# 512 rows of wq on 64 partitions, eight rows to a partition, contracted in eight steps of 64

## The chip, the cores and the metric

The kernel runs on one core of a Trainium2 chip. The core has five instruction streams: PE (TensorE, matmuls and their weight loads), DVE (VectorE), ACT (ScalarE), POOL (GpSimd) and SP (SyncE, which here issues nearly all loads). Sixteen DMA engines move data between the chip's memory (HBM) and SBUF, the 128-partition working memory. Matmuls read SBUF and write PSUM. The metric is the device time of one execution in microseconds (us).

## The reference: one decode step of a transformer block

Four sequences, one new token each, D = 576 features. The block is attention with a cached window and then a gated feed-forward layer, each behind a layer norm:

```python
q = (layernorm(x) @ wq)                      # [4, 576] @ [576, 32*128]
k = k_cache[:, :, Sk-4096:, :]               # 16 KV heads, 2 query heads for each
v = v_cache[:, :, Sk-4096:, :]
p = softmax(q . k * 128**-0.5)
h = x + (p . v) @ wo
h2 = h + (relu(hn @ W_gate) * (hn @ W_up)) @ W_down     # hn = layernorm(h)
```

Everything is bfloat16. The caches' windows are 4 x 16 x 4096 x 128 values each, 67 MB for K and 67 MB for V; wq and wo have 4.7 MB each, the three matrices of the feed-forward layer 5.3 MB each. Some 160 MB are read for each execution. This case is about the first product, layernorm(x) @ wq, and about how wq is brought into SBUF.

## The kernel before, in words

**Recording.** There is no automatic scheduler. Each engine's program is a Python function (`prog_sync`, `prog_act`, `prog_dve`, `prog_pe`, `prog_pool`), and an instruction is given the names of those it depends on. The class `Sched` runs all programs twice: first to number the names, then to emit, where a name becomes a wait on a semaphore's value. The order on an engine is the order written in its function. A wait that an engine has already made for the same or a higher value of the same counter is left out.

**SBUF as a pool.** All large loads go to one buffer, `pool`, of 65,536 bfloat16 columns on 128 partitions (128 KB each), used as four slots of `QUAD` = 16,384 columns. One K or V "quad" is four KV heads of one sequence, 4096 KB, and fills a slot: 128 partitions x 32 KB. There are 16 quads of K and 16 of V. `add` (line 203) puts a load on the list `transfers` and works out which earlier users of the same columns it has to wait for. K and V take the slots in turn, in the order K0, K1, V0, K2, V1, K3, ... (line 238): K0 has slot 0, K1 slot 1, V0 slot 2, K2 slot 3, V1 slot 0 again. The weights wo, W_gate, W_up and W_down come after the last V.

**The order of loads.** `prog_sync` issues `transfers` in order on SP's queue, one after the other, and waits ahead of each for the users of its columns. The first entries are the last 64 rows of wq (line 234, 512 KB, two half rows on 128 partitions, at the start of slot 3), the first 512 rows of wq (line 236, 4096 KB, all of slot 2), then the K and V quads. Since slots 0 and 1 are free at the start, K0 and K1 are issued without a wait. V0 (slot 2) and K2 (slot 3) wait for "QMM", the last matmul with wq. V1 waits until K0 has been transposed, and so on.

**The product with wq.** Partition p holds rows 4p to 4p+3 of wq (512 rows as 128 x 4). The normalized x, `xn_bf` (4 x 576), is turned by PE with five transposes (`turn`, line 473; `feat(c)` picks the features c, c+4, c+8, ...), and ACT copies the result to `xnT` (line 311, features 0 to 511) and `x4` (line 310, the last 64). A small matmul with `dup` spreads the last 64 over 128 partitions ("XDUP", line 480). Then the loop of line 481 goes over the row steps c: first c = 4, the last 64 rows, which need only the smaller load, then c = 0 to 3, each contracting over 128 partitions. For each c there are eight matmuls of 512 columns (4 groups g of 32 PSUM partitions, 2 banks k). The groups g write different 32-column strips of the array. A matmul with k = 1 is emitted without a weight load of its own (`held`). Line 464 is the matmul with a weight load and line 466 the held one; all matmuls of the kernel are recorded at these two lines, so in a profile they are told apart by their tiles.

**After the product.** ACT copies q to SBUF (line 320). DVE transposes the first part of K0 (line 402), then q (line 428). PE rearranges q, ACT builds the block-diagonal weights `qz` (line 336), and the loop over quads begins: four transposes of K on DVE, the scores on PE, the maximum on DVE, its reduction over partitions on POOL, the exponential on ACT, the transpose of the probabilities on DVE, and the product with V on PE.

Of the kernel before, what the change touches and what calls it, by code (L numbers as in the profile page):

```python
# [10 lines left out]
BF16 = mybir.dt.bfloat16  # L11

B = 4
D = 576
# [7 lines left out]
DC = 5  # L22
# [9 lines left out]
QUAD = NS * WIN * DH // 128  # L32
# [70 lines left out]
def bass_sequential_preLN__sliding_block_cached__glu_gated_reglu__decode_kernel(  # L103
# [12 lines left out]
    with ExitStack() as es:  # L116
        cnt = [0]

        def sb(name, shape, dt):
            return es.enter_context(nc.sbuf_tensor(name, shape, dt))  # L120

        pool = sb("pool", [128, NSLOT * QUAD], BF16)
        kT = sb("kT", [128, NKT, QUAD // 8], FP32)
        ident_b = sb("ident_b", [128, 128], BF16)
# [6 lines left out]
        x_bf = sb("x_bf", [B, D], BF16)  # L131
        xn_bf = sb("xn_bf", [B, D], BF16)
        st1 = sb("st1", [B, 20], FP32)
        xnT = sb("xnT", [128, 4, 32], BF16)
        xn4 = sb("xn4", [128, 2, 32], BF16)
        x4 = sb("x4", [64, B], BF16)
        dup = sb("dup", [64, 128], BF16)
# [37 lines left out]
        pb = [sc[:, i * 512:(i + 1) * 512] for i in range(4)]  # L175
# [4 lines left out]
        QB = (5, 6)  # L180
# [13 lines left out]
        tpv = pb[TPB].bitcast(BF16)  # L194

        S = Sched()
# [4 lines left out]
        at = {}  # L201

        def add(name, key, off, n, consumer, make):

            free = []
            for u in list(users):
                if u[0] < off + n and off < u[1]:
                    if u[2] not in free:
                        free.append(u[2])
                    if off <= u[0] and u[1] <= off + n:  # L210
                        users.remove(u)
            users.append((off, off + n, consumer))
            at[name] = off
            transfers.append((name, key, free, lambda e: make(e, pool[:, off:off + n])))
# [12 lines left out]
        def add_V(i):  # L227
# [3 lines left out]

        HQ = H * DH

        add(("wq", 4), "wq4", 2 * QUAD + 4 * HQ, HQ // 2, "QMM",
            lambda e, o: e.dma_start(out=o, in_=A_wq[512:576, :].rearrange("r (u n) -> (r u) n", u=2)))
        add(("wq", 0), "wq0", 2 * QUAD, 4 * HQ, "QMM",
            lambda e, o: e.dma_start(out=o, in_=A_wq[0:512, :].rearrange("(p u) n -> p (u n)", u=4)))
        for m in range(NQUAD + VLEAD):
            if m < NQUAD:
                add_K(m)  # L240
# [4 lines left out]
        for k, (kind, W) in enumerate((("wg", B_W_gate), ("wu", B_W_up))):  # L245
            add((kind, 0), f"{kind}0", GU0 + 4 * k * ROW, 4 * F, None,
                lambda e, o, W=W: e.dma_start(out=o, in_=W[0:512, :].rearrange("(p u) n -> p (u n)", u=4)))
            add((kind, 4), f"{kind}4", GU0 + 8 * ROW + k * HALF, HALF, None,
                lambda e, o, W=W: e.dma_start(out=o, in_=W[512:576, :].rearrange("r (u n) -> (r u) n", u=2)))
# [3 lines left out]
        for k, (f0, f1) in enumerate(WD):  # L253
            transfers.append((("wd", k), f"wd{k}", ["ATTN"],
                              lambda e, f0=f0, f1=f1: e.dma_start(
                                  out=pool[:, f0 * D:f1 * D], in_=B_W_down.rearrange("(p j) n -> p (j n)", j=JJ)[:, f0 * D:f1 * D])))

        def feat(c):
            return slice(c, c + 509, 4) if c < 4 else slice(512, D)

        def land(name):
            return ("L",) + (name if isinstance(name, tuple) else (name,))
# [38 lines left out]
        def prog_act(S):  # L301
            a = "scalar"
            S.dma(a, lambda e: e.dma_start(out=x_bf[:, :], in_=A_x.rearrange("b s d -> (b s) d")), "x", name=land("x"))
            S.op(a, lambda e: e.activation(out=st1[:, 14:15], in_=st1[:, 13:14], func=ACT.Sqrt, bias=eps_c[0:B, 0:1], scale=1.0),
                 deps=["D_VAR", "EPS"], name="A_STD")
            S.op(a, lambda e: e.copy(out=dup[:, :].rearrange("p (r u) -> p r u", u=2),
                                     in_=bass.AP(tensor=ident_b, offset=0, ap=[[128, 64], [1, 64], [0, 2]])), deps=["IDB"], name="DUP")
            S.op(a, lambda e: e.copy(out=col[:, :].rearrange("p (a s) -> p a s", s=NS),
                                     in_=bass.AP(tensor=ident_b, offset=0, ap=[[128, NS], [0, 128], [1, NS]])), name="COL")
            S.op(a, lambda e: e.copy(out=x4[:, :], in_=tpv[0:64, 16:20]), deps=["TP1"], name="D_X4")  # L310
            S.op(a, lambda e: e.copy(out=xnT[:, :, 0:B], in_=tpv[:, 0:16].rearrange("p (c b) -> p c b", b=B)), deps=["XNZ"], name="D_XNT")
            S.op(a, lambda e: e.activation(out=foe[:, :].rearrange("p (a s x) -> p a s x", s=NS, x=2),
                                           in_=bass.AP(tensor=ident_b, offset=0, ap=[[128, NS], [0, 16], [1, NS], [0, 2]]),
                                           func=ACT.Copy, scale=FAR, bias=-FAR), name="FOE")
            S.op(a, lambda e: e.activation(out=mask[:, 1, :], in_=mask[:, 0, :], func=ACT.Copy, scale=FAR, bias=-FAR), deps=["M0"], name="M1")
            for u in range(2):
                S.op(a, lambda e, u=u: e.activation(out=xn4[:, u, 0:B], in_=pb[STB][:, 0:B], func=ACT.Copy, scale=par[:, u:u + 1]),
                     deps=["XDUP", "PAR2", "XN4Z"], name=f"XN4{u}")
            for k in range(2):
                S.op(a, lambda e, k=k: e.copy(out=q_bf[:, k, :].rearrange("p (x e k) -> p x e k", e=2, k=32),  # L320
                                              in_=pb[QB[k]].rearrange("p (x k e) -> p x e k", e=2, k=32)), deps=["QMM"], name=f"QBF{k}")
            S.op(a, lambda e: e.copy(out=qrep[:, :, :].rearrange("p x (g y) -> p x g y", g=4),  # L322
                                     in_=sc.ap().rearrange("p (g r) -> p g r", g=4)[:, :, 0:128].rearrange("p g (x y) -> p x g y", x=4)),
                 deps=["QREP"], name="D_QR")
# [16 lines left out]
            for i in range(NQUAD):  # L341
                S.op(a, lambda e, i=i: e.activation(out=pmax[:, i % 2, :], in_=mask[:, 1, :], func=ACT.Identity, bias=rmx[:, i % 2:i % 2 + 1], scale=1.0),  # L342
                     deps=[("RMAX", i)], name=("EMAX", i))
                deps = [("BIAS", i)]
                if i >= 2:
                    deps.append(("TRP", i - 2))
                S.op(a, lambda e, i=i: e.activation(  # L347
                    out=Pb[:, (i % 2) * 1024:(i % 2 + 1) * 1024], in_=sc[:, (i % 2) * 1024:(i % 2 + 1) * 1024], func=ACT.Exp,
                    scale=SCALE, bias=bias[:, i % 2:i % 2 + 1], accum_out=rs1[:, i:i + 1]),
                    deps=deps, name=("EXP", i))  # L350
                if i + 2 < NQUAD:
                    qzero(i + 2)
            S.op(a, lambda e: e.copy(out=bass.AP(tensor=spread, offset=0, ap=[[16 * H, H], [4 * H + 1, 4], [4, H]]),
                                     in_=bass.AP(tensor=ident_b, offset=0, ap=[[128, H], [0, 4], [1, H]])),
                 deps=["SP0"], name="SPREAD")
            S.op(a, lambda e: e.copy(out=oX[:, :, :].rearrange("p e b -> p (e b)"), in_=pb[0][:, 0:EO * B]), deps=["OSEL"], name="OX")  # L356
            S.op(a, lambda e: e.activation(out=st2[:, 14:15], in_=st2[:, 13:14], func=ACT.Sqrt, bias=eps_c[0:B, 0:1], scale=1.0),
                 deps=["D_VAR2"], name="A_STD2")
            S.op(a, lambda e: e.copy(out=hnT[0:64, 4, 0:B], in_=tpv[0:64, 16:20]), deps=["TP2", "HN4Z"], name="N1")
            S.op(a, lambda e: e.copy(out=hnT[:, 0:4, 0:B], in_=tpv[:, 0:16].rearrange("p (c b) -> p c b", b=B)), name="N2")  # L360
            for u in range(2):
                S.op(a, lambda e, u=u: e.activation(out=hn4[:, u, 0:B], in_=pb[SUB][:, 400:400 + B], func=ACT.Copy, scale=par[:, u:u + 1]),
                     deps=["HDUP"], name=f"HN4{u}")
            for k, (f0, f1) in enumerate(CUTS):
                S.op(a, lambda e, k=k, f0=f0, f1=f1: e.activation(out=gate_sb[:, :, f0:f1].rearrange("p j f -> p f j"), in_=part(0, k, "f j"), func=ACT.Relu),
                     deps=[("GATE", k)], name=("RELU", k))
# [90 lines left out]
        def prog_pe(S):  # L457
            t = "tensor"

            def mm(o, l, r, start, stop, deps=(), name=None, skip=False, held=False):  # L460

                def make(e):
                    if not held:
                        return e.matmul(o, lhsT=l, rhs=r, start=start, stop=stop, skip_group_check=skip)  # L464
                    tile = tuple(next(x for x in (32, 64, 128) if x >= n) for n in (l.shape[0], l.shape[-1]))
                    return e.add_instruction(mybir.InstMatmult(  # L466
                        name=nc.get_next_instruction_name(), start_tensor_calc=start, stop_tensor_calc=stop, bass_skip_group_check=skip,
                        tile_size=tile, tile_position=(0, o.offset // o.ap[0][0] % 128), ldweights=False,
                        ins=[e.lower_ap(r), e.lower_ap(l)], outs=[e.lower_ap(o)]))

                S.op(t, make, deps=deps, name=name, signal=name is not None)

            def turn(src, deps, name):
                for c in range(DC):
                    w = 128 if c < 4 else 64
                    S.op(t, lambda e, c=c, w=w: e.transpose(out=tpv[0:w, c * 4:(c + 1) * 4], in_=src[0:B, feat(c)], identity=ident_b[0:B, 0:B]),
                         deps=deps if c == 0 else [], name=name if c == DC - 1 else None, signal=c == DC - 1)

            turn(xn_bf, ["XN", "IDB"], "TP1")
            mm(pb[STB][:, 0:B], dup[:, :], x4[:, :], True, True, deps=["D_X4", "DUP"], name="XDUP")  # L480
            for c in (4, 0, 1, 2, 3):
                s = at[("wq", 0)] + c * HQ if c < 4 else at[("wq", 4)]
                deps = [land(("wq", 0)), "D_XNT"] if c == 0 else [land(("wq", 4)), "XN41"] if c == 4 else []
                for g in range(4):
                    x0 = s + (g if c < 4 else g % 2) * 1024
                    for k in range(2):
                        mm(pb[QB[k]][32 * g:32 * g + 32, :], xnT[:, c, :] if c < 4 else xn4[:, g // 2, :], pool[:, x0 + 512 * k:x0 + 512 * k + 512], c == 4, c == 3,
                           deps=deps, name="QMM" if c == 3 and g == 3 and k == 1 else None, skip=True, held=k == 1)
                        deps = []
            for g in range(4):  # L490
                mm(pb[g][:, 0:128].rearrange("p (x h b) -> p x h b", x=4, b=B), sel[32 * g:32 * g + 32, :, :].rearrange("p g k -> p (g k)"),
                   qT[32 * g:32 * g + 32, :].rearrange("p (h x b) -> p x h b", x=4, b=32)[:, :, :, 0:B], True, True,
                   deps=["D_QT", "SEL"] if g == 0 else [], name="QREP" if g == 3 else None)
# [50 lines left out]
            for q in range(4):  # L544
                mm(pb[0][:, 0:EO * B], spread[:, q, :, :].rearrange("p h k -> p (h k)"), o_bf[:, q * EO:(q + 1) * EO, :].rearrange("p e b -> p (e b)"), q == 0, q == 3,
                   deps=["NORM", "SPREAD"] if q == 0 else [], name="OSEL" if q == 3 else None)
            for e_ in range(EO):
                deps = [land(("wo",)), "OX"] if e_ == 0 else []
                for u in range(2):
                    c0 = at[("wo",)] + e_ * D + u * HD  # L550
                    mm(attn[:, u * HD:(u + 1) * HD], oX[:, e_, :], pool[:, c0:c0 + HD], e_ == 0, e_ == EO - 1,
                       deps=deps, name="ATTN" if e_ == EO - 1 and u == 1 else None, held=u == 1)
                    deps = []
# [10 lines left out]
            for u, kind in ((0, "wg"), (1, "wu")):  # L564
                if u == 1:
                    residual()
                for c in range(4):
                    s = at[(kind, 0)] + c * F
                    deps = [land((kind, 0))] + (["N2"] if c == 0 and u == 0 else [])
                    for k, (f0, f1) in enumerate(CUTS):  # L570
                        for q in range(4):
                            x0 = s + q * FQ
                            mm(pb[GUB[u][k]][32 * q:32 * q + 32, 0:(f1 - f0) * JJ], hnT[:, c, :], pool[:, x0 + f0 * JJ:x0 + f1 * JJ],
                               c == 0, False, deps=deps, skip=True, held=k > 0)
                            deps = []
                s = at[(kind, 4)]
                deps = [land((kind, 4)), "HN41"]
                for k, (f0, f1) in enumerate(CUTS):
                    for q in range(4):
                        x0 = s + (q % 2) * FQ  # L580
                        mm(pb[GUB[u][k]][32 * q:32 * q + 32, 0:(f1 - f0) * JJ], hn4[:, q // 2, :], pool[:, x0 + f0 * JJ:x0 + f1 * JJ],
                           False, True, deps=deps, name=(("GATE", "GU")[u], k) if q == 3 else None, skip=True, held=k > 0)
                        deps = []

            for k, (f0, f1) in enumerate(WD):
                deps = [land(("wd", k))]
                for f in range(f0, f1):
                    if f % (JJ // 2) == 0:
                        deps = deps + [("HHT", f // (JJ // 2))]
                    for u in range(2):  # L590
                        last = f == FC - 1
                        mm(down(u), hhT[:, f, 0:B], wd_sb[:, f, OUTS[u][0]:OUTS[u][1]], False, last,
                           deps=deps, name="DOWN1" if last and u == 1 else None, skip=True)
# [37 lines left out]
```

## Time and profile before

| What | Value |
|---|---|
| median of 3 timed runs | 377.9 us (377.59 to 378.06) |
| profiled execution | 378.37 us |
| its span, first to last instruction | 377.0 us |
| mean granted TensorE clock | 0.923 |
| PE busy | 291.9 us (77%) |
| DVE busy | 222.5 us (59%) |
| ACT busy | 53.1 us (14%) |
| DMA, SP's queue | 159.59 MB, 98.7% of 16 engines' span |
| mean rate of all DMA | 424 GB/s |
| first 512 rows of wq, issue to landing | 13.6 us |
| last 64 rows of wq, issue to landing | 3.3 us |

Times in the profile are in us from the start of the span, unless marked ns. L236 means line 236 of the kernel. A line of the timeline has the start, the duration, the engine, the line, the operation, what it writes and reads, the count, and in brackets how long the engine was idle before and what ended that. The windows give, for stretches of the span, the busy time of each engine with the number of its instructions, the granted clock of TensorE, the mean busy share of the 16 DMA engines, and what they moved in GB/s. The share can pass 1.00 a little, because a packet is counted where it ends. SPq stands for DMA issues on SP. "Issue" time of a load and its landing are told apart: a load is issued in half a microsecond and lands when its last packet has.

### The profile page before, as it was taken

The numbers are of one execution on the slowest core, as the hardware profiler recorded it, in microseconds if no ns is written. First come the engines' busy times: TensorE is split into PE (matmuls) and PEld (weight loads), VectorE is DVE, ScalarE is ACT, GpSimd is POOL, SyncE is SP. The second block draws the span as 40 slices with busy tenths as digits, with TensorE's granted clock in tenths as the row PEclk, the third lists the DMA queues.
The fourth block names the chain that finished last, engine by engine and source line by source line (L and its number), as shares of the span: only waits on it lengthen the run. The fifth ranks groups of instructions, "written<-read, shape, count | busy, mean of one in ns | idle before, by whom it ended". The sixth has DMA issues, their size and how long they took to land.

```text
span 377.0 us, 2565 instructions
## 1 busy us (share of the span) xinstructions
PE 291.9 (77%) x1384; PEld 67.9 (18%) x740; DVE 222.5 (59%) x169; ACT 53.1 (14%) x138; POOL 12.1 (3%) x34
## 2 busy tenths in 40 slices
PE   1408299969996999499939996799689967977675
PEld 0001012212221222022202221122112211222213
DVE  3037577696859494859476856775676658221230
ACT  3003402010220012001200220021002010101020
POOL 6000000000000000000000000000000000000000
PEclk9999879998998799989998998999869995996989
DMA  8999999999999999999999999999999999999995
GB/s 334 431 445 441 403 438 440 441 418 424 437 441 428 414 441 436 435 410 441 441 426 421 435 445 428 431 422 441 431 435 415 441 435 428 447 428 416 418 417 245
DMA packets 6507, 159.74 MB, mean 424 GB/s; under 512 B 729, under 2 KB 865, under 8 KB 1633
## 3 DMA queue, kind: packets, MB, share of 16 engines
q1 hardware_dynamic: 6488, 159.59, 98.7%
q8 instruction: 8, 0.13, 0.1%
q14 instruction: 3, 0.02, 0.0%
q10 hardware_dynamic: 8, 0.00, 0.0%
HBM read 159.58 MB, written 0.00 MB: 423 GB/s over the span
## 4 chain that ended last, share of the span: by engine, by line
DMA 53%; DVE 28%; PE 15%; ACT 2%; issue 1%; SPq 1%; POOL 0%; DVEq 0%
DMA pool<-in_A_k_cache_dram 48%; DVE kT L402 19%; PE sc L464 5%; PE sc L466 5%; DMA pool<-in_B_W_down_dram 5%; DVE acc L421 4%; DVE own_sb L418 2%; PE val L464 2%; PE val L466 2%; DVE probT L415 1%; DVE rmx L405 1%; ACT P L347 1%; DVE o_bf L440 0%; ACT L347 0%; ACT qz L336 0%
## 5 line engine op out<-in xcount | busy, mean ns | idle before, releaser
L402 DVE STREAM_TRANSPOSE kT<-pool 128x2048 f32<-128x2048 f32 x64 | 142.9, 2279 | 34.9 <-DMA pool<-in_A_k_cache_dram 33.9
L464 PE MATMUL sc<-kT,qz 128*128 128x512 bf16 x240 | 104.4, 435 | 28.7 <-DVE kT L402 28.7
L466 PE MATMUL sc<-kT,qz 128*128 128x512 bf16 x256 | 110.4, 431 | 18.3 <-DVE kT L402 16.2
L464 PE MATMUL val<-pool,probT 128*64 128x512 bf16 (+2 forms) x328 | 102.4, 360 | 4.6 <-DMA pool<-in_B_W_down_dram 4.6
L466 PE MATMUL val<-pool,probT 128*64 128x512 bf16 x256 | 96.2, 379 | 0.0
L464 PEld LDWEIGHTS sc<-kT,qz 128*128 128x128 bf16 x256 | 26.9, 105 | 154.8 <-issue 76.3
L464 PEld LDWEIGHTS val<-pool,probT 128*64 128x64 bf16 (+1 forms) x328 | 31.4, 104 | 88.0 <-issue 78.1
L405 DVE TENSOR_REDUCE rmx<-sc 128x1 f32<-128x1024 f32 x16 | 19.6, 1225 | 42.4 <-PE sc L466 42.4
L342 ACT ACTIVATE pmax<-mask,rmx 128x8 f32<-128x8 f32 x16 | 4.8, 301 | 241.3 <-DVE rmx L405 241.3
L415 DVE STREAM_TRANSPOSE probT<-P 128x1024 bf16<-128x1024 bf16 x16 | 19.9, 1245 | 20.7 <-ACT P L347 20.7
L347 ACT ACTIVATE P<-sc,bias 128x1024 bf16<-128x1024 f32 x16 | 17.8, 1113 | 13.3 <-DVE bias L410 13.3
L336 ACT COPY qz<-qrep 32x128 bf16<-32x128 bf16 x64 | 18.8, 294 | 0.6
L294 POOL PARTITION_ALL_REDUCE bcm<-pmax x16 | 5.9, 367 | 312.8 <-ACT pmax L342 312.8
L421 DVE TENSOR_REDUCE acc<-own_sb 128x128 f32<-128x1024 f32 x8 | 15.2, 1895 | 0.3
L418 DVE TENSOR_TENSOR own_sb<-val,mask 128x1024 f32<-128x1024 f32 x8 | 9.5, 1193 | 8.3 <-PE val L466 8.3
L464 PE MATMUL sc<-pool,oX 128*4 128x288 bf16 x32 | 10.2, 345 | 0.4 <-ACT oX L356 0.4
L408 DVE SCALAR_TENSOR_TENSOR t<-bcm,mask 128x8 f32<-128x8 f32 x16 | 2.7, 167 | 13.3 <-POOL bcm L294 13.3
L466 PE MATMUL sc<-pool,oX 128*4 128x288 bf16 x32 | 10.2, 343 | 0.0
L464 PE MATMUL sc<-qT,sel 32*128 32x128 bf16 x4 | 0.3, 284 | 9.8 <-DVE qT L428 9.8
L443 DVE TENSOR_TENSOR h_row<-sc,x_bf 4x576 f32<-4x576 f32 x1 | 0.7, 745 | 11.9 <-PE sc L466 11.9
L464 PE MATMUL sc<-col,foe 4*128 4x512 bf16 x16 | 6.4, 399 | 0.7 <-ACT qrep L322 0.7
L464 PE MATMUL val<-pool,xnT 128*32 128x512 bf16 x16 | 2.6, 628 | 5.0 <-DMA pool<-in_A_wq_dram 5.0
(98 smaller groups left out, 74.4 us busy)
## 6 DMA issues: line engine op xcount, KB each, us to landing
pool<-in_A_k_cache_dram SPq DMA_DIRECT2D x16, 4096.0 KB, 26.9
pool<-in_A_v_cache_dram SPq DMA_DIRECT2D x16, 4096.0 KB, 26.8
pool<-in_A_wo_dram SPq DMA_DIRECT2D x1, 4608.0 KB, 18.3
pool<-in_B_W_gate_dram SPq DMA_DIRECT2D x1, 4608.0 KB, 17.8
pool<-in_B_W_up_dram SPq DMA_DIRECT2D x1, 4608.0 KB, 24.0
pool<-in_A_wq_dram SPq DMA_DIRECT2D x1, 4096.0 KB, 13.6
pool<-in_B_W_down_dram SPq DMA_DIRECT2D x1, 2016.0 KB, 13.7
pool<-in_B_W_down_dram SPq DMA_DIRECT2D x1, 1296.0 KB, 16.4
```

What stands on the lines that cost most here:

```text
L294: S.op(g, lambda e, i=i: e.partition_all_reduce(bcm[:, i % 2, :], pmax[:, i % 2, :], 128, bass_isa.ReduceOp.max), deps=deps, name=("PAR", i))
L336: S.op(a, lambda e, src=src, dst=dst: e.copy(out=dst, in_=src), deps=deps, name=("QZ", i) if g == 3 else None, signal=g == 3)
L342: S.op(a, lambda e, i=i: e.activation(out=pmax[:, i % 2, :], in_=mask[:, 1, :], func=ACT.Identity, bias=rmx[:, i % 2:i % 2 + 1], scale=1.0 ...
L347: S.op(a, lambda e, i=i: e.activation(out=Pb[:, (i % 2) * 1024:(i % 2 + 1) * 1024], in_=sc[:, (i % 2) * 1024:(i % 2 + 1) * 1024], func=ACT ...
L402: S.op(v, lambda e: e.transpose(out=dst, in_=src), deps=deps, name=("TR", f))
L405: S.op(v, lambda e: e.tensor_reduce(out=rmx[:, i % 2:i % 2 + 1], in_=sc[:, (i % 2) * 1024:(i % 2 + 1) * 1024], axis=AX.X, op=ALU.max), dep ...
L408: S.op(v, lambda e: e.scalar_tensor_tensor(out=t8[:, :], in0=bcm[:, i % 2, :], scalar=-SCALE, in1=mask[:, 0, :], op0=ALU.mult, op1=ALU.mul ...
L415: S.op(v, lambda e: e.transpose(out=pT[i % NPT], in_=Pb[:, (i % 2) * 1024:(i % 2 + 1) * 1024]), deps=[("EXP", i)] + ([("PV", i - NPT)] if ...
L418: S.op(v, lambda e: e.tensor_tensor(out=own_sb[:, :].rearrange("p (x d) -> p x d", d=DH), in0=val[:, :].rearrange("p (x d) -> p x d", d=DH ...
L421: S.op(v, lambda e: e.tensor_reduce(out=acc[:, w % 2, :], in_=own_sb[:, :].rearrange("p (x d) -> p d x", d=DH), axis=AX.X, op=ALU.add), de ...
L464: return e.matmul(o, lhsT=l, rhs=r, start=start, stop=stop, skip_group_check=skip)
L466: return e.add_instruction(mybir.InstMatmult(name=nc.get_next_instruction_name(), start_tensor_calc=start, stop_tensor_calc=stop, bass_ski ...
```

## The change

The first 512 rows of wq go to 64 partitions in place of 128. Partition p (0 to 63) holds rows 8p to 8p+7, which is 64 KB for a partition: the load (still one DMA of 4096 KB) now takes slots 2 and 3 of the pool, on their lower 64 partitions. The last 64 rows, which lay at the start of slot 3, move to the start of slot 1. By the bookkeeping of `add`, K1, which goes to slot 1, now has to wait for the last matmul with wq; V0 and K2 have to wait for the same matmul, as before.

The product goes over eight steps of 64 partitions in place of four of 128: 64 matmuls of 512 columns where there were 32, after the eight with the last 64 rows. `turn` gets a parameter `u`, the number of rows to a partition, and makes nine transposes of 64 features here in place of five (the second use, behind the second layer norm, keeps five). `xnT` is 64 x 8 x 32 in place of 128 x 4 x 32, and ACT's two copies read other columns of the transposes' PSUM bank. `feat` falls away, and with it three lines, so that line numbers behind it are three lower.

```diff
-        xnT = sb("xnT", [128, 4, 32], BF16)
+        xnT = sb("xnT", [64, 8, 32], BF16)
...
-        add(("wq", 4), "wq4", 2 * QUAD + 4 * HQ, HQ // 2, "QMM",
+        add(("wq", 4), "wq4", QUAD, HQ // 2, "QMM",
...
-        add(("wq", 0), "wq0", 2 * QUAD, 4 * HQ, "QMM",
-            lambda e, o: e.dma_start(out=o, in_=A_wq[0:512, :].rearrange("(p u) n -> p (u n)", u=4)))
+        add(("wq", 0), "wq0", 2 * QUAD, 8 * HQ, "QMM",
+            lambda e, o: e.dma_start(out=o[0:64, :], in_=A_wq[0:512, :].rearrange("(p u) n -> p (u n)", u=8)))
...
-            S.op(a, lambda e: e.copy(out=x4[:, :], in_=tpv[0:64, 16:20]), deps=["TP1"], name="D_X4")
-            S.op(a, lambda e: e.copy(out=xnT[:, :, 0:B], in_=tpv[:, 0:16].rearrange("p (c b) -> p c b", b=B)), deps=["XNZ"], name="D_XNT")
+            S.op(a, lambda e: e.copy(out=x4[:, :], in_=tpv[0:64, 32:36]), deps=["TP1"], name="D_X4")
+            S.op(a, lambda e: e.copy(out=xnT[:, :, 0:B], in_=tpv[0:64, 0:32].rearrange("p (c b) -> p c b", b=B)), deps=["XNZ"], name="D_XNT")
...
+            def turn(src, deps, name, u=4):
+                for c in range(u + 1):
+                    w = 512 // u if c < u else 64
+                    cols = slice(c, c + 512 - u + 1, u) if c < u else slice(512, D)
...
-            turn(xn_bf, ["XN", "IDB"], "TP1")
+            turn(xn_bf, ["XN", "IDB"], "TP1", u=8)
...
-            for c in (4, 0, 1, 2, 3):
+            for c in (8, 0, 1, 2, 3, 4, 5, 6, 7):
...
+                np_ = 64 if c < 8 else 128
...
-                        mm(pb[QB[k]][32 * g:32 * g + 32, :], xnT[:, c, :] if c < 4 else xn4[:, g // 2, :], pool[:, x0 + 512 * k:x0 + 512 * k + 512], c == 4, c == 3,
+                        mm(pb[QB[k]][32 * g:32 * g + 32, :], xnT[:, c, :] if c < 8 else xn4[:, g // 2, :], pool[0:np_, x0 + 512 * k:x0 + 512 * k + 512], c == 8, c == 7,
```

More of the change, by code (lines that the diff above doesn't have):

```diff
@@ L256, in bass_sequential_preLN__sliding_block_cached__glu_gated_reglu__decode_kernel @@
                                   out=pool[:, f0 * D:f1 * D], in_=B_W_down.rearrange("(p j) n -> p (j n)", j=JJ)[:, f0 * D:f1 * D])))
-        def feat(c):
-            return slice(c, c + 509, 4) if c < 4 else slice(512, D)
         def land(name):
@@ L471, in mm @@
                 S.op(t, make, deps=deps, name=name, signal=name is not None)
[L473 to L477, printed above, removed]
-            turn(xn_bf, ["XN", "IDB"], "TP1")
+            def turn(src, deps, name, u=4):
+                for c in range(u + 1):
+                    w = 512 // u if c < u else 64
+                    cols = slice(c, c + 512 - u + 1, u) if c < u else slice(512, D)
+                    S.op(t, lambda e, c=c, w=w, cols=cols: e.transpose(out=tpv[0:w, c * 4:(c + 1) * 4], in_=src[0:B, cols], identity=ident_b[0:B, 0:B]),
+                         deps=deps if c == 0 else [], name=name if c == u else None, signal=c == u)
@@ L480, in prog_pe @@
+            turn(xn_bf, ["XN", "IDB"], "TP1", u=8)
             mm(pb[STB][:, 0:B], dup[:, :], x4[:, :], True, True, deps=["D_X4", "DUP"], name="XDUP")
-            for c in (4, 0, 1, 2, 3):
-                s = at[("wq", 0)] + c * HQ if c < 4 else at[("wq", 4)]
-                deps = [land(("wq", 0)), "D_XNT"] if c == 0 else [land(("wq", 4)), "XN41"] if c == 4 else []
+            for c in (8, 0, 1, 2, 3, 4, 5, 6, 7):
+                s = at[("wq", 0)] + c * HQ if c < 8 else at[("wq", 4)]
+                deps = [land(("wq", 0)), "D_XNT"] if c == 0 else [land(("wq", 4)), "XN41"] if c == 8 else []
+                np_ = 64 if c < 8 else 128
@@ L484, in prog_pe @@
                 for g in range(4):
-                    x0 = s + (g if c < 4 else g % 2) * 1024
+                    x0 = s + (g if c < 8 else g % 2) * 1024
                     for k in range(2):
-                        mm(pb[QB[k]][32 * g:32 * g + 32, :], xnT[:, c, :] if c < 4 else xn4[:, g // 2, :], pool[:, x0 + 512 * k:x0 + 512 * k + 512], c == 4, c == 3,
-                           deps=deps, name="QMM" if c == 3 and g == 3 and k == 1 else None, skip=True, held=k == 1)
+                        mm(pb[QB[k]][32 * g:32 * g + 32, :], xnT[:, c, :] if c < 8 else xn4[:, g // 2, :], pool[0:np_, x0 + 512 * k:x0 + 512 * k + 512], c == 8, c == 7,
+                           deps=deps, name="QMM" if c == 7 and g == 3 and k == 1 else None, skip=True, held=k == 1)
```

## The prediction

> **What bounds the kernel now.** I read the page first (slices, chain of waits, DMA issues), then the timeline of the first 25 us, the windows of the stages and the list of DMA issues.
>
> ```profile
> DMA  8999999999999999999999999999999999999995
> GB/s 334 431 445 441 403 438 440 441 418 424 437 441 428 414 441 436 435 410 441 441 426 421 435 445 428 431 422 441 431 435 415 441 435 428 447 428 416 418 417 245
> q1 hardware_dynamic: 6488, 159.59, 98.7%
> ```
>
> The 16 DMA engines are busy from the first slice to the last, and the rate stays between 403 and 447 GB/s whatever is loaded. The kernel is bound by its loads: what delays one of them delays the end, unless a later stretch has room. The windows show none.
>
> ```profile
> 24.00:30.00 6.00, 1.12 (x6) 0.21 (x5) 5.31 (x4) 1.41 (x4) 0.00 (x0) 1.00 1.01 437
> 30.00:36.00 6.00, 5.37 (x17) 1.12 (x9) 4.97 (x3) 1.56 (x6) 0.00 (x0) 1.00 1.00 431
> 222.00:228.00 6.00, 6.00 (x30) 1.43 (x13) 2.08 (x4) 2.58 (x7) 0.37 (x1) 1.00 0.98 421
> 360.00:366.00 6.00, 4.77 (x80) 0.61 (x24) 1.49 (x3) 2.15 (x3) 0.00 (x0) 0.83 1.02 431
> ```
>
> The last two numbers are the DMA share and the rate: 0.98 to 1.02 early, in the middle and near the end. The prices of the steps come from the start of the timeline (start, duration, what; in brackets the idle time ahead and who ended it):
>
> ```profile
> 1.18 0.41 SPq L237 DMA_DIRECT2D pool<-in_A_wq_dram  x1
> 1.64 1.32 SPq L225 DMA_DIRECT2D pool<-in_A_k_cache_dram  x2
> 7.27 0.42 PE L476 MATMUL pb<-ident_b,xn_bf 4*128 4x4 bf16 x5 [7.27 <-DVE xn_bf L380]
> 14.81 0.62 PE L464 MATMUL val<-pool,xnT 128*32 128x512 bf16 x4 [5.04 <-DMA pool<-in_A_wq_dram]
> 15.21 0.65 PE L466 MATMUL pb<-pool,xnT 128*32 128x512 bf16 x4
> 18.48 0.54 SPq L230 DMA_DIRECT2D pool<-in_A_v_cache_dram  x1
> 24.69 2.31 DVE L402 STREAM_TRANSPOSE kT<-pool 128x2048 f32<-128x2048 f32 x1 [17.48 <-DMA pool<-in_A_k_cache_dram]
> ```
>
> wq's 512 rows land at 14.8, the first K at 24.7. PE needs 3.67 us for the product with those rows, and only then (18.48) does SP issue the first V. Two K loads, issued at 1.64, keep the queue full meanwhile. The first idle of PE ahead of that product (5.0 us) is a wait for the load.
>
> **The change, part by part.** The durations are of the profiled execution: 378.37 us, its span 377.0 and 1.37 around it; the median of the three timed runs is 377.9, 0.47 lower. The difference found is added to the median.
>
> *The load of 512 rows into 64 partitions.* It is the same 4096 KB, 64 rows of 64 KB in place of 128 rows of 32 KB. No load of before has this shape. Price of such a load at the plateau: in the chain of waits the DVE takes up every second K from 113.10 to 307.40 us at steps of 38.86 us, four loads of 4096 KB each, so 9.71 us for one, 432 GB/s, 27 GB/s for each engine. All these loads do two things at once: use 16 engines and fill 128 partitions. If the engines set the plateau, the new load costs the same 9.71 us (+0). If the destination partitions set it, half of them take half the rate: 19.4 us (+9.7). To choose, I look at the only load into few partitions, x (4 rows of 1152 B, on the ACT queue), in the DMA view of 1.2 to 2.2 us:
>
> ```profile
> q10 hardware_dynamic: 8, 0.00, 2.2%
> ```
>
> Eight packets for four rows: four of data and four of under 512 B, which I read as one completion for each engine used. So rows are dealt out anew over the engines, and 64 rows can have 16 of them. Their time is 2.2% of 16 engines in 1 us, 0.35 us for 4608 B: 13 GB/s for a busy engine, 0.48 of the plateau's 27. The packets are short, which costs by itself, so this row is weak; but it lies at the half end, and I take that end: **+9.7**. The other end, +0, is a rival. Upwards, if doubling applies to all the time between the landing of wq's last 64 rows (issued at 0.72, 3.3 us to landing: 4.0) and that of the 512 (14.8), it is +10.8. Downwards: from 2 to 15 us the DMA view has 303 packets, 147 of them under 8 KB; of the other 156, 128 are wq's, so 28 of the first K were already through when wq had only just landed, 1.75 for an engine at 1.2 us each; if slower engines share the longer load with faster ones and this 2.1 us of unevenness goes, +7.6.
>
> The Trainium skill speaks against the change here: SBUF — State Buffer, section "Door 1: The DMA port swizzle", says that partitions 0 to 63 reach only 8 of the 16 ports that DMA writes go through, and gives 196 GB/s for 1 MiB into 64 partitions beside 328 into 128, with 218 GB/s as the limit of large ones. By that limit this load would take an estimated 19.2 us, 9.5 more, so 387.4 us by the page; no run so far shows it.
>
> *The first K waits behind it* on the same queue and lands 9.7 later; so do its transposes, the first product with K, and everything after. Everything that takes up a later load is released by these, so the pipeline is moved as a whole.
>
> *64 products of 64 rows in place of 32 of 128.* In the rows above, four run beside one another (four of L464, then four of L466, 0.425 us apart): 32 take 8 such rounds, 3.4 us, and 0.25 to the end. After: 16 rounds. All at that pace: 6.8 + 0.25 = 7.1 us. In the first three stretches of K products the pace doubled after 5.1, 4.0 and (at 315 us) 6.1 us; with 4.0 it is 5.7 us. The 16 more weight loads (0.10 to 0.15 us) lie under the products. I take 6.3, 2.6 longer than now. Who waits: the copies of q (0.58 and 0.59 us, ending at 19.55), which are needed by the transpose of q at 26.93, behind the first K on the DVE: 7.4 us of cover, 4.8 left. It costs nothing.
>
> *The second K is issued later.* Its slot now holds the last 64 rows of wq, so SP's fourth DMA waits for the product, and the first V and third K, which waited for it before, stand behind. Their order is unchanged, and three issues at 0.54 us are soon done. What is late is the second K: issued at 1.64 + 0.67 before, now 6.3 after wq's landing. The engines have the first K until 9.9 after that landing (24.69 - 14.81). From issue to the first packet it takes about 1.0 us (0.72 to the first packets after 1.6). So 6.3 + 1.0 = 7.3 against 9.9: covered by 2.6 on the slowest engine, but engines that are 2.1 ahead have only 0.5 of cover. If the product takes the full 7.1, these are idle for 0.3; the slowest, which sets the landing, is not. I take **+0.1**, bounds 0 and +0.7. The cover holds whether or not the load is slow, since both count from its landing.
>
> *The rest is hidden.* Nine transposes of xn for five: four more at 0.084 us, 0.34; the product with the last 64 rows then ends near 10.1 in place of 9.8, 4.7 us before even the old landing. The clearing of xnT, 256 columns for 128 (0.20 us now, 0.51 for 512 columns): about +0.1 on POOL, whose next results (xn4 cleared at 5.3, wanted at 8.16) have 2.8 us. The two copies out of the transposes stay at 0.15 and 0.17 us. Without the wait for wq's load these would add 0.5 us.
>
> Sum: 9.7 + 0.1 = 9.8; 378.37 + 9.8 = 388.2 for a profiled execution, **387.7** beside the median of 377.9.
>
> **The rivals.**
>
> *The engines set the plateau, not the partitions: no change.* wq lands at 14.8 as now, the second K's wait is covered, and the longer rows save a little: a 4 KB packet takes 0.4 us x 16 / 37 = 0.173 us between 2.6 and 3.0 us against 0.151 at the plateau, 0.02 for a packet, four fewer on each engine. 377.8 to 378.6. For it: the plateau is the same for rows of 32 and of 36 KB, and 16 engines are used either way. Against: the x load above. It decides "same" if the load takes under 10.4 us (403 GB/s). Faster, under 377.1, would need nine times the saving on packets (0.09 us); no row offers that.
>
> *The products of 64 rows don't run four at a time.* Then 64 x 0.425 = 27.2 us of product; the second K starts 27.2 + 1.0 after wq's landing, where the first ended at 9.9: 18.3 us of empty queue, 377.9 + 9.7 + 18.3 = 405.9. It would cost from 8.9 us of product on. Against it: the four of a round differ in the columns of the array (32 each), which the change leaves alone.
>
> *In part: the rate lies between half and full*, say three quarters (324 GB/s): 12.9 us, +3.2, 381.2. Nothing in the profile points to such a value.
>
> **How the numbers follow.** Half rate 0.86 (the x row, though its packets are short); no change 0.08; between 0.03; products one at a time 0.03. The half-rate case runs from 377.9 + 7.6 = 385.5 to 377.9 + 10.8 + 0.7 = 389.4. Holding that, the range leaves out the other cases, 0.14, and a little of its own. Within 0.2% (0.76 us, about what a measurement can tell from no change) lie 0.07 of the second case, faster 0.01 of it; the rest is slower: 0.92.
>
> **What would show it.** Right: the first product with the 512 rows starts near 24.5 in place of 14.8; PE is then busy with them for 5.7 to 7.1 us; SP issues the second K right at their end, near 31; the DVE starts on the first K near 34.4; DMA moves near 216 GB/s between 4 and 24 us and the old plateau afterwards; every later landing is some 9.8 later. Wrong: a start at 14.8 (no change), a first K much earlier than 9.9 us after wq (the engines overlap the two), an empty queue after the first K, or a later stretch that gives time back.

## The result and the profile after

The changed kernel takes 389.63 us (five runs, 389.47 to 391.33), the kernel before 378.01 us: 1.032 times as long (95% interval 1.030 to 1.035), 11.6 us more. The direction of the forecast holds, and so does the chain from a late load to a late end; the size does not: 387.7 was forecast, with a range up to 389.4.

The page of the changed kernel, its slices (40 of 9.75 us; busy share of the DMA engines in tenths, and their rate):

```profile
DMA  9979999999999999999999999999999999999996
GB/s 249 215 232 380 430 428 430 430 430 431 428 428 430 430 430 428 430 430 430 430 432 430 430 430 428 430 437 434 434 430 428 430 430 430 434 433 425 441 405 259
```

The whole loss is in the first four slices. In the first three of them the DMA engines are busy at about half the rate; from the fifth slice on the plateau of before is back. No later stretch gives anything back and none loses more.

The start of its timeline (start, duration, what; line numbers are three lower than before from `feat` on):

```profile
1.77 32.84 SPq L225 DMA_DIRECT2D pool<-in_A_k_cache_dram  x2
9.85 0.67 PE L463 MATMUL pb<-pool,xn 128*32 128x512 bf16 x4
27.00 0.62 PE L461 MATMUL val<-pool,xnT 64*32 64x512 bf16 x4 [16.49 <-DMA pool<-in_A_wq_dram]
33.38 0.65 PE L463 MATMUL pb<-pool,xnT 64*32 64x512 bf16 x4
34.09 0.58 ACT L317 CAST q_bf<-val 128x512 bf16<-128x512 f32 x1 [24.77 <-PE pb L463]
34.66 0.61 SPq L230 DMA_DIRECT2D pool<-in_A_v_cache_dram  x1
36.45 2.31 DVE L399 STREAM_TRANSPOSE kT<-pool 128x2048 f32<-128x2048 f32 x1 [29.23 <-DMA pool<-in_A_k_cache_dram]
```

PE now waits 16.5 us for the 512 rows of wq, which land at 27.0 (14.8 before). The product takes 7.1 us, to 34.09. The issues of K0 and K1 stand in one row, from 1.77 to 34.61: K1 goes out behind the product. K0 is taken up at 36.45 (24.69 before).

Three windows of the changed kernel (length, busy time of PE, PEld, DVE, ACT and POOL, granted clock, DMA share, GB/s):

```profile
3.00:3.50 0.50, 0.00 (x0) 0.00 (x0) 0.50 (x2) 0.00 (x0) 0.50 (x1) 1.00 7.60 1770
8.00:8.50 0.50, 0.43 (x5) 0.35 (x4) 0.00 (x0) 0.03 (x1) 0.00 (x0) 1.00 5.12 1049
34.00:36.00 2.00, 0.03 (x4) 0.00 (x0) 0.00 (x0) 1.07 (x2) 0.00 (x0) 1.00 0.50 164
```

Two from the kernel before:

```profile
10.50:11.00 0.50, 0.00 (x0) 0.00 (x0) 0.00 (x0) 0.00 (x0) 0.00 (x0) 1.00 2.12 918
34.00:36.00 2.00, 2.00 (x10) 0.42 (x4) 1.94 (x1) 0.00 (x0) 0.00 (x0) 1.00 0.87 377
```

In so short a window a packet is counted whole. 1049 GB/s for 0.5 us are 8 packets of 64 KB; they take 5.12 x 0.5 x 16 = 41 us together, 5.12 us each, 12.8 GB/s for an engine. The first window shows that a packet is counted where it begins (not where it ends, as the section on the profile before has it): it holds 885 KB, most of them in packets of 64 KB, and none of these, issued at 1.17 or later, can have ended by then. Before, 14 packets of 32 KB take 1.21 us each, 27.0 GB/s. An engine carries four such rows now and carried eight before: 20.5 us against 9.7. The last window of the changed kernel is the gap behind K0: a share of 0.50 between 34 and 36 us.

### The profile page after: what moved, and what is told of

The parts are those of the page before. It is cut to its first block, busy times and chain, and to the rows that moved or that the text cites. A ratio compares the mean times of both kernels' runs of the same rounds, so it can differ in the third digit from the quotient of the medians.

```text
span 390.0 us, 2637 instructions
## 1 busy us (share of the span) xinstructions
PE 299.8 (77%) x1436; PEld 69.7 (18%) x760; DVE 222.6 (57%) x169; ACT 53.0 (14%) x138; POOL 12.2 (3%) x34
## 4 chain that ended last, share of the span: by engine, by line
DMA 55%; DVE 27%; PE 14%; ACT 2%; SPq 1%; issue 1%; POOL 0%; DVEq 0%
DMA pool<-in_A_k_cache_dram 50%; DVE kT L399 18%; PE sc L461 5%; DMA pool<-in_B_W_down_dram 5%; PE sc L463 5%; DVE acc L418 4%; DVE own_sb L415 2%; PE val L461 2%; PE val L463 2%; DVE probT L412 1%; DVE rmx L402 1%; ACT P L344 1%; DVE o_bf L437 0%; ACT L344 0%; ACT qz L333 0%
## 5 line engine op out<-in xcount | busy, mean ns | idle before, releaser
L461 PE MATMUL sc<-kT,qz 128*128 128x512 bf16 x256 | 110.6, 432 | 44.5 <-DVE kT L399 44.2
L463 PE MATMUL sc<-kT,qz 128*128 128x512 bf16 x256 | 109.8, 429 | 0.0
L461 PE MATMUL val<-pool,probT 128*64 128x512 bf16 (+2 forms) x328 | 103.8, 372 | 4.3 <-DMA pool<-in_B_W_down_dram 4.2
L461 PEld LDWEIGHTS val<-pool,probT 128*64 128x64 bf16 (+1 forms) x328 | 32.2, 107 | 88.3 <-issue 78.1
L461 PE MATMUL val<-pool,xnT 64*32 64x512 bf16 x32 | 5.1, 628 | 16.5 <-DMA pool<-in_A_wq_dram 16.5
L474 PE MATMUL pb<-ident_b,xn_bf 4*64 4x4 bf16 x9 | 1.2, 248 | 7.3 <-DVE xn_bf L377 7.3
## 6 DMA issues: line engine op xcount, KB each, us to landing
pool<-in_A_v_cache_dram SPq DMA_DIRECT2D x16, 4096.0 KB, 26.9
```

Source lines behind the costliest of these rows:

```text
L463: return e.add_instruction(mybir.InstMatmult(name=nc.get_next_instruction_name(), start_tensor_calc=start, stop_tensor_calc=stop, bass_ski ...
```

## The experiments

Each kernel ran beside the kernel before on the same chip; times are medians. Three questions: does the load's price come from the partitions that are written, from their number, or from the long rows; what does K1's wait cost; and where is the rest of the 11.6 us.

**K1's wait taken away (e1).** The last 64 rows of wq go to a part of `kT` that is free until after the product.

```diff
-        add(("wq", 4), "wq4", QUAD, HQ // 2, "QMM",
-            lambda e, o: e.dma_start(out=o, in_=A_wq[512:576, :].rearrange("r (u n) -> (r u) n", u=2)))
+        w4 = kT[:, 2, :].bitcast(BF16)
+        transfers.append((("wq", 4), "wq4", [],
+                          lambda e: e.dma_start(out=w4[:, 0:HQ // 2], in_=A_wq[512:576, :].rearrange("r (u n) -> (r u) n", u=2))))
...
```

> The changed kernel with one thing undone: the last 64 rows of wq go to a buffer that is free until the third transpose of K0, so slot 1 is free and K1 is issued at the start again. Theory 1 (all the loss is in the load of 512 rows; K1's wait is covered as forecast): the time stays at 389.5, within 0.4. Theory 2 (the load costs 10.4, four packets of 5.0 us on an engine, and the rest is an empty queue between K0 and K1, where the trace shows a DMA share of 0.50 from 34 to 36 us): 388.0 to 388.6, and the two groups of times seen for the changed kernel (389.5 and 391.3) become one.

389.26 us (388.72 to 390.19), the kernel before 378.03; the unedited changed kernel beside it (after_again) 389.67. The difference of 0.4 us is inside the scatter of both. So some 11.2 us stay without the wait: theory 1's 389.5, within 0.4, holds, and theory 2's 388.0 to 388.6 is missed. The window of e1 shows the gap gone:

```profile
34.00:36.00 2.00, 0.15 (x4) 0.00 (x0) 0.00 (x0) 1.07 (x2) 0.00 (x0) 1.00 1.15 492
```

Its timeline has K0 taken up at

```profile
36.58 2.31 DVE L400 STREAM_TRANSPOSE kT<-pool 128x2048 f32<-128x2048 f32 x1 [29.36 <-DMA pool<-in_A_k_cache_dram]
```

which is as late as in the changed kernel, and the span ends at 388.9, 352.3 us after that. The kernel before has 377.0 - 24.69 = 352.3 as well. The changed kernel has 390.0 - 36.45 = 353.6, and 353.1 in its other two profiles. So by this measure the gap costs 0.8 to 1.2 us, and e1's way from K0's landing to the end is as before.

**K1's wait alone, with a short and with a long product (e2, e3).** e2 is the kernel before with one edit; e3 adds a second pass over the four steps (the part of q from the first 512 rows is doubled), so the product has as many matmuls as the changed kernel's, behind a load at the old rate.

```diff
-        add(("wq", 4), "wq4", 2 * QUAD + 4 * HQ, HQ // 2, "QMM",
+        add(("wq", 4), "wq4", QUAD, HQ // 2, "QMM",
...
-            for c in (4, 0, 1, 2, 3):
+            for n_, c in enumerate((4, 0, 1, 2, 3, 0, 1, 2, 3)):
...
```

> The kernel before with K1's wait alone: the last 64 rows of wq at the start of slot 1, so K1 waits for the product, which keeps its 32 matmuls. Both theories: K1 is issued 3.7 us after wq's landing, 5 us before K0 ends; 378.0, within 0.4. If the wait costs by itself, 378.5 to 380.

> The kernel of e2 with the 32 matmuls of the first 512 rows made twice (their part of q is doubled), so the product is as long as the changed kernel's (7.1 us) and the load is the old one. Theory 1: K1 is issued 7.1 us after wq's landing, K0 ends 9.9 after it; 378.0 to 378.4. Theory 2: the engines that are ahead run empty for 1 to 1.5 us; 379 to 380.

e2: 377.92 us, 1.000 times the kernel before (0.999 to 1.001). The wait costs nothing behind a short product. e3: 379.2 us as a median of two groups: six of twelve runs from 377.67 to 378.76, six from 379.64 to 379.98. Its profile is of the fastest run:

```profile
14.52 0.62 PE L464 MATMUL val<-pool,xnT 128*32 128x512 bf16 x4 [4.74 <-DMA pool<-in_A_wq_dram]
17.05 0.54 PE L464 MATMUL val<-pool,xnT 128*32 128x512 bf16 x4
17.42 0.39 PE L466 MATMUL pb<-pool,xnT 128*32 128x512 bf16 x4
19.59 0.54 SPq L225 DMA_DIRECT2D pool<-in_A_k_cache_dram  x1
```

Here PE's pace doubles in the round that begins at 17.05 us (afterwards a matmul takes 0.39 us in place of 0.65), the product ends after 5.1 us, not the 7.1 that was planned, and nothing is lost. The slower group would then be runs in which the pace did not rise.

**The same with PE kept busy until wq lands (e8).**

```diff
+            for _ in range(14):
+                mm(pb[0][0:32, :], xn4[:, 0, :], pool[:, at[("wq", 4)]:at[("wq", 4)] + 512], True, True, deps=[land(("wq", 4)), "XN41"])
             for n_, c in enumerate((4, 0, 1, 2, 3, 0, 1, 2, 3)):
...
```

> The kernel of e3 (K1 waits, product twice) with 14 unused matmuls on PE between 9 us and the landing of wq, so that PE runs at its faster pace when the product begins: 3.5 to 4 us in place of 5.1 to 7.1. If the two groups of e3's times (377.7 to 378.8 and 379.6 to 380.0) are products at the faster and the slower pace, whose K1 comes earlier or later: all runs 377.7 to 378.4. If the groups have another cause: both groups again.

378.15 us (377.89 to 379.03), 1.000 times the kernel before (0.9995 to 1.001); the upper group is gone. The product starts at 14.39 and K1 is issued at 18.08, after 3.7 us. So K1's wait costs nothing behind 3.7 or 5.1 us of product. The 1.7 us of e3's upper group go with the slower pace; no profile caught such a run, so that it takes 7.1 us there is inferred.

**One more load, three destinations (e4, e5, e6).** The kernel before, with one load of 1792 KB (1.835 MB) of V's unused part between wq and K0. It fills a free part of slot 3, and only K2 waits for it.

```diff
+        add(("extra",), "extra", 3 * QUAD + 2048, 14336, ("L", "extra"),
+            lambda e, o: e.dma_start(out=o[0:64, :], in_=A_v_cache[0, 0, 0:7168, :].rearrange("(p t) d -> p (t d)", t=112)))
```

This is e5; e6 has `o[32:96, :]`, and e4 `o[0:128, :]` with half the columns and t=56.

> The kernel before with one more load between wq's 512 rows and K0, nothing waits for it but K2 (its slot): 1792 KB (1.835 MB) into 128 partitions, 14 KB each. At the plateau of 432 GB/s it costs 4.25 us: 382.2.

> The same 1792 KB into partitions 0 to 63, 28 KB each (rows shorter than the 32 KB of the K loads). If 64 low partitions take half the rate, or the 13.1 GB/s of an engine that the changed kernel's trace shows: 8.5 to 8.8 us, 386.5 to 386.8. If the long rows of 64 KB were the cause in the changed kernel, and not the partitions: 382.2.

> The same 1792 KB into partitions 32 to 95, 28 KB each. If the number of partitions sets the rate: as e5, 386.5 to 386.8. If it is which partitions (by the Trainium skill, SBUF — State Buffer, section Door 1: The DMA port swizzle, 32 to 95 reach all 16 ports and 0 to 63 only 8): as e4, 382.2.

The kernel before beside them: 377.93 us. e4 382.19 (+4.26), e5 387.48 (+9.55), e6 382.08 (+4.15). e5 lies above the 386.5 to 386.8 expected, which counted on 13.1 GB/s for an engine where the windows of the changed kernel give 12.8. Two windows in which e5's load runs, and one of e6's:

```profile
14.50:15.00 0.50, 0.00 (x0) 0.00 (x0) 0.00 (x0) 0.00 (x0) 0.00 (x0) 1.00 1.40 287
16.00:20.00 4.00, 3.37 (x32) 0.55 (x16) 0.00 (x0) 0.56 (x2) 0.00 (x0) 1.00 1.05 215
```

```profile
14.00:14.50 0.50, 0.12 (x4) 0.11 (x4) 0.00 (x0) 0.00 (x0) 0.00 (x0) 1.00 1.60 688
```

In e5 5 packets of 28 KB take 2.24 us each, 12.8 GB/s for an engine; in e6 12 take 1.07 us each, 26.9 GB/s.

This settles the cause: which partitions are written. 64 partitions from 32 to 95 take this load as fast as all 128; 64 partitions from 0 to 63 take it at 215 GB/s, with rows of 28 KB, shorter than K's. It is neither the number of partitions nor the long rows. By the Trainium skill (SBUF — State Buffer, "Door 1: The DMA port swizzle"), 0 to 63 share 8 of 16 ports and 32 to 95 reach all 16; the three times agree with its map, though no trace here shows a port. Its limit of 218 GB/s is not reached: e5's load costs 9.55 us, 192 GB/s, 2.24 times e4's and not twice.

**The changed kernel on partitions 32 to 95 (e7), and its load in two (e10, e11).** e7 is e1 with the 512 rows on partitions 32 to 95. Two tiles of 32 rows are needed for each step, so the product is made in halves.

```diff
-            lambda e, o: e.dma_start(out=o[0:64, :], in_=A_wq[0:512, :].rearrange("(p u) n -> p (u n)", u=8)))
+            lambda e, o: e.dma_start(out=o[32:96, :], in_=A_wq[0:512, :].rearrange("(p u) n -> p (u n)", u=8)))
...
+            steps = [(c, 0) for c in range(8)] + [(8, 0)] + [(c, 1) for c in range(8)]
...
```

e10 is the changed kernel, and e11 is e7, with rows of 32 KB in two DMAs:

```diff
+        for x in range(2):
+            add(("wq", x), f"wq{x}", (2 + x) * QUAD, 4 * HQ, "QMM",
+                lambda e, o, x=x: e.dma_start(out=o[0:64, :], in_=A_wq[0:512, :].rearrange("(p x u) n -> p x (u n)", x=2, u=4)[:, x, :]))
...
```

> The kernel of e1 (K1 not waiting) with the same 512 rows of wq, eight to a partition, on partitions 32 to 95 in place of 0 to 63; the product is made in two halves of 32 partitions, so it is longer, 8 to 14 us, which is covered because K1 is in the queue. If which partitions are written is the whole price of the load: wq lands near 14.5 us and the time is 378.0, within 0.5, where e1 has 389.3. If 64 KB rows or the halved number of partitions still cost something in this kernel: over 379.

> The changed kernel with the load of the 512 rows in two DMAs, the first four of each partition's eight rows and then the other four, so rows of 32 KB as for K in place of 64 KB, on the same partitions 0 to 63; the product still waits for both. If the loss beyond the forecast half (11.2 for the load in place of 9.7) comes from sharing a port by two engines: unchanged, 389.7, within 0.6. If it comes from the long rows: 387.7 to 388.3.

> The kernel of e7 (partitions 32 to 95) with the load in the same two DMAs. In e7 wq landed at 16.8 us and K0 at 26.5, 2 us later than in the kernel before. If the rows of 64 KB cost these 2 us: K0 lands at 24.3 to 24.7 and the time is 378.0 to 378.9. If not: 380.7 again.

e7: 380.7 us (+2.7, forecast +0). It takes 8.6 us off e1's 389.26, but not all. e11: 380.65 (+2.8), wq at 17.04 and K0 at 26.68: shorter rows change nothing there. e10: 390.94 (389.39 to 392.41, +13.1), above both of its forecasts and no gain from shorter rows. A window and a line of its timeline:

```profile
10.50:11.00 0.50, 0.02 (x3) 0.00 (x0) 0.00 (x0) 0.00 (x0) 0.00 (x0) 1.00 3.53 721
34.51 2.31 DVE L400 STREAM_TRANSPOSE kT<-pool 128x2048 f32<-128x2048 f32 x1 [27.29 <-DMA pool<-in_A_k_cache_dram]
```

The window holds 11 packets of 32 KB, 2.57 us each: 12.8 GB/s again. K0 is taken up 1.9 us earlier than in the changed kernel, 9.8 later than in the kernel before, yet the span is 388.7, 354.2 us after that: what K0 gains is lost behind it. K1 waits here too, and how much of the loss is its, is open. So when K0 is taken up does not by itself tell what such a load costs.

What is left in e7 (timeline):

```profile
16.84 0.62 PE L464 MATMUL val<-pool,xnT 32*32 32x512 bf16 x4 [8.37 <-DMA pool<-in_A_wq_dram]
26.54 2.31 DVE L402 STREAM_TRANSPOSE kT<-pool 128x2048 f32<-128x2048 f32 x1 [19.32 <-DMA pool<-in_A_k_cache_dram]
33.33 1.25 DVE L428 STREAM_TRANSPOSE qT<-q_bf 128x1024 bf16<-128x1024 bf16 x1 [4.48 <-ACT q_bf L320]
```

wq still lands 2.0 us later than in the kernel before (16.84 against 14.81), and K0 1.9 later; and since the product takes 15.4 us here, the DVE waits 4.5 us for q, which the edit brought in. Between 2 and 8 us 380 GB/s move at a DMA share of 1.05, where the kernel before has 428 at 1.03, so packets are slower in that stretch. Why wq lands 2 us later on these partitions, where the extra load of e6 cost nothing, is open.

**The changed kernel with PE kept busy (e9), and unedited (after_again, after_third).** As e8, with 70 unused matmuls ahead of the changed kernel's product.

> The changed kernel with 70 unused matmuls on PE until wq lands, so that its product takes 3.5 to 4 us in place of 7.1; K1 still waits for it. If the gap between K0 and K1 costs 0.4 to 1.2 us: 388.7 to 389.3, as e1, and no time over 390.5. If the gap costs nothing: 389.7 as before.

> The changed kernel once more, unedited, for the two groups of its times. Theory 1: 389.5 is the rule and 391.3 the exception, without a difference in the first 40 us. Theory 2: executions differ in how long the product takes (5.7 us where the TensorE's pace rises in it, 7.1 where not), so in when K1 is issued; a profile of the faster group shows the product at 5.7 to 6.5 us and less of a dip between 34 and 36 us.

> The changed kernel unedited, beside e9 on the same chip: 389.6, within 0.5, by both theories; the difference to e9 is the price of the gap.

e9: 391.19 us (390.89 to 392.71), later than either theory had it and than the changed kernel beside it (after_third), 390.3 (389.67 to 391.13), which itself lies over the 389.6 expected. The product takes 3.7 us as intended, but wq lands at 27.30 and K0 at 37.02, the latest of all; from there to the end it is 352.9 us, 0.2 to 0.7 less than in the changed kernel and 0.6 more than in the kernel before, though K1 is issued 6 us before K0 has landed. So its time doesn't price the gap. Measured by the way from K0 to the end, against e9, the gap would cost 0.2 to 0.7 us and not 0.8 to 1.2. Why e9's load is late is open. after_again: 389.67 (389.07 to 390.42). Neither theory's account of the two groups of times holds: the product takes 7.1 us in all three profiles. Their K0 is taken up at 36.45, 35.37 and 36.66 us and their spans are 390.0, 388.5 and 389.8: what differs between executions is mostly the load itself, by about 1.2 us.

## Why the prediction was right or wrong, point by point

- **What bounds the kernel: right.** From K0's landing on, e1 and the kernel before need the same 352.3 us, so what e1's start loses is seen at the end; e10, with 354.2, loses more behind K0.
- **The choice of the half rate: near in size, in part by luck, and wrong in its reason.** The row it rested on, four short packets of x, was weak. The forecast read the limit as one that goes with the number of partitions ("half of them take half the rate"); e6 fills 64 partitions at the full rate. e5 against e6 shows that it is which partitions are written, and it excludes the first rival (the engines alone set the plateau): with the changed load they are busy, at 12.8 GB/s in place of 27.0. The rival of a rate between half and full fell too: it is below half.
- **The load's price of +9.7: the term that was mis-sized.** e1, which has this load without the gap, measured +11.2 us. The rate is not half but less: 5.12 us for a 64 KB packet where half the plateau's rate gives 4.85. Four packets are 20.5 us against 9.7, +10.8; the 0.4 us beyond that are not in the packets' pace, and where they come from is open. e5 alone, 9.55 - 4.26 = 5.29 us for 1.835 MB, scaled to 4.19 MB, gives an estimate of +12.1. The upper bound of +10.8 was worked out from a landing doubled, not from a rate below one half; that the packets give the same figure is chance, and the bound was too low.
- **The 64 products: half right.** Four still run beside one another, so the second rival (one at a time) fell. Their duration was put at 6.3 us, from K products whose pace rose after 4.0 to 6.1 us; it was 7.1, because the pace never rose. q was still ready in time: its copies end at 35.16, its transpose starts at 38.68.
- **K1's wait, +0.1: probably too small.** The step counted on the slowest engine, which the gap does not reach. Against e1 and the kernel before, the traces price the gap at 0.8 to 1.2 us, against e9 at 0.2 to 0.7, and e1's median at 0.4 with scatter. The 28 packets of K0 that the forecast took as through by 15 us had only begun, by the way packets are counted, so that some engines are 2.1 us ahead was not measured. e2 and e8 show that the wait is free behind a shorter product; e3's upper group, 1.7 us up, is where it is not. Which engine's loss moves the end was not seen in any view.
- **The rest is hidden: right.** The nine transposes cost 1.16 us in place of 0.42 (an estimate of 0.34 more became 0.74), and the product with the last 64 rows ends at 10.5, with 16.5 us to spare.

Together, by the medians: 11.2 for the load and 0.4, inside the scatter, for the gap make the 11.6 measured, in place of 9.7 and 0.1.

## What to carry to other kernels

A load's price depends on which partitions it writes: here 0 to 63 took a load at less than half the rate, and 32 to 95 at the rate of all 128. A kernel that is bound by its loads pays that in full, even for a single load of 2.6% of its bytes at the very start. When a buffer moves, look also at what now waits for its release: the same wait was free behind 3.7 and 5.1 us of matmuls, and behind 7.1 the profiles show a gap in the loads that cost an estimated 0.2 to 1.2 us.

## What the runs showed of the hardware that was not expected

Partitions 0 to 63 cost a load more than half of its rate: an engine moves 12.8 GB/s there, with packets of 64, of 32 (e10) and of 28 KB (e5), and e5's whole load 192 GB/s, against 27.0 for an engine in a load that fills all 128.

TensorE's pace did not rise by itself under products that fill few rows of the array. With 128 rows it doubled after 2.5 us in e3's profile, though not within the 3.7 us of the kernel before. With 64 rows it stayed at 0.43 us a round for the whole 7.1 us in all three profiles of the changed kernel, and in e7, with 32 rows, for nearly all of 15 us. In e9, where PE came in at the faster pace, products of 64 rows kept it for their 3.7 us. Three rounds of the second half of e7's product, which begins at 25.15, an early one and the last two (timeline):

```profile
26.40 0.64 PE L466 MATMUL pb<-pool,xnT 32*32 32x512 bf16 x4
31.09 0.64 PE L464 MATMUL val<-pool,xnT 32*32 32x512 bf16 x4
31.52 0.64 PE L466 MATMUL pb<-pool,xnT 32*32 32x512 bf16 x4
```

The granted clock in the windows reads 1.00 all the while, so this column does not tell the two paces apart. The Trainium skill (TensorE: Matmul & The Clock Gate, "Part 1: The HAM clock gate") has the pace rise after about 3.4 us of sustained work; in e3 it rose after 2.5 us, while in the products of 64 and of 32 rows it did not rise. That the number of rows is the reason was not tested by itself.
